# Routing records that leave the order of visits to the reader, with memsets of 128x256 words between the scatters

## The chip, the cores and the metric

One core of one Trainium2 chip runs the whole program. The metric is device time in microseconds (us) per run; fewer is better. A profiled execution is a run of its own with the hardware profiler on: its span goes from the first to the last instruction, and its own time lies a little above the span.

## The reference, cut to what matters

Two layers follow each other. The first is attention over keys and values that are averaged in groups of 8, the second a mixture of 8 experts, of which each token visits two.

```python
def _attn_ref(q, k, v):                      # q, k, v: (8, 8, 576, 64)
    k_p = k.reshape(B, H, Sp, pool, D).mean(axis=3)      # pool = 8, Sp = 72
    v_p = v.reshape(B, H, Sp, pool, D).mean(axis=3)
    scores = scale * np.matmul(q, k_p.transpose(0, 1, 3, 2))
    attn = softmax(scores)
    return np.matmul(attn, v_p)

def _moe_ref(x, w_gate, w_noise, noise, w1, w2):   # x: (4608, 512), E, F = 8, 1024
    noisy_logits = x @ w_gate + np.log1p(np.exp(x @ w_noise)) * noise
    top2 = the two largest of noisy_logits per token
    top2_w = softmax over these two
    for e in range(E):
        for k in range(2):
            mask = top2[:, k] == e
            h = np.maximum(x[mask] @ w1[e], 0.0)
            out[mask] += top2_w[mask, k, None] * (h @ w2[e])

reference: x = attention output as (4608, 512); out = _moe_ref(x, ...)
```

## The kernel before

**Attention and router.** The 8 batches are taken as 4 pairs of 1152 tokens each. A pair's x rows are stored in `x_dram`, and while the next pair's attention runs, the router `route` (L506 to L676) works out the top two experts of the pair before: their weights, and for each choice its position in the expert's list (L629 casts it). It then writes a record of four words per choice into `rec_dram`: the number of the x row, the weight, the row of `out` or a number out of bounds (L647), and the slot of the other visit (L643). Here each token's visits have an order: only the second one, in the order of the experts, adds the first one's result, which lies in `slot_dram`, and writes the sum to `out`. The dozen operations at L630 to L647 find that order from both choices.

**Scatters.** A pair has 9 columns of 128 tokens and two choices, so 18 indirect DMAs (`scatter`, L649) of 128 records each, on GpSimd's queue (POOL). They are kept in a list, `scq`, in program order with what follows them: the loading of records (`load_recs`, L678) and the gathers of x rows (`fetch`, L744). `advance(n, m)` (L794) takes m of them from the list at places in the attention and in the first groups of the experts, and ties them to a recent instruction (`pace`). `quiet` keeps some of these places free. `spaced` (L496) puts a memset of `spacer`, 128x512 words, between any two indirect DMAs:

```python
            with tc.issue_after(tail_ind[0].ins):
                gap = nc.gpsimd.memset(spacer[0], 0.0)
            with tc.issue_after(gap.ins):
                tail_ind[0] = make()
```

For the last scatters the memsets go to the buffer `lg3`, which has the same size.

**Experts.** An expert's list is cut into groups of up to four tiles of 128 tokens. For expert 0 they are tiles 0 to 3 (group 0), 4 and 5 (group 1) and 6 to 9 (group 2); group 3 is the first of expert 1. Group 0 needs records of pairs 0 and 1 alone, group 1 those up to pair 2, group 2 those up to pair 3, so these three are loaded apart, as `raw0_0`, `raw0_4` and `raw0_6`, and all records of experts 1 to 7 as `raw1_0`. The first two of these loads go out on POOL, the rest on SP's queue, which also carries the x rows and the weight loads `wst` (L459). The list `scq` has, after pair 2's scatters, `raw0_4` and the gathers of group 1, then pair 3's scatters, `raw0_6` and the gathers of group 2.

Each group runs through the same steps. Its rows are gathered (`xg`, L718) and transposed (on PE for expert 0, L768) and split into a high and a low part (`split`); stage 1 multiplies by w1 (L1030, with L1041 on ScalarE and L1042 on VectorE, which split h again), stage 2 by w2 (L1141 for expert 0, or L1107) tile by tile. Then `finish` scales a tile's rows by the weight (L1080, L1078) into one of three buffers `pv` and stores them in `slot_dram` (L1082, on POOL) or scatters them to `out` (L1086). The split of the next group stands after a tile of the group's stage 2, by `hook` (L1178): after tile 1 - i of group i. In front of the groups' code three memsets fill the `pv` buffers (L981).

**Engines.** PE is TensorE, DVE is VectorE, ACT is ScalarE, POOL is GpSimd, SP is SyncE. Each runs its own queue in order; the order is that of the program, with the pins of `issue_after`.

## Time and profile before

| What | Value |
| --- | --- |
| median of 3 runs | 1026.51 us (1026.15 to 1030.2) |
| profiled execution, its own time | 1030.06 us |
| its span | 1028.1 us |
| PE busy | 994.1 us (97%) |
| PE weight loads | 890.1 us (87%) |
| DVE busy | 551.6 us (54%) |
| ACT busy | 345.0 us (34%) |
| POOL busy | 415.1 us (40%) |
| chain that ended last, PE's share | 79% |

The profiled execution is 3.55 us above the median. Busy times are sums over the span; work on different engines overlaps. A wait in the timeline is the idle time ahead of an instruction with what released it. The attention ends at about 190 us; from there the program is the groups of the experts one after another.

### The profile page before, as it was taken

Reading aid. Unit: us, or ns where it says so; the run is one execution under the profiler, and the core shown is the slowest. Engines: PE = TensorE matmul, PEld = TensorE weight load, DVE = VectorE, ACT = ScalarE, POOL = GpSimd, SP = SyncE. Lnnn points to the kernel's source line nnn. Section 1 sums busy time; section 2 is a strip of 40 time slices with the busy share of each in tenths; the row PEclk is TensorE's granted clock in tenths of the full one; section 3 lists DMA queues with packets and bytes.
Section 4 is the critical chain, followed back from the end, with each engine's and each line's share of the span. In section 5 each row is a group of like instructions: output and inputs, shape, how many; then the busy total and the mean of one; then the engine's idle time right before and its main releaser. Section 6 shows DMA issues by size and latency. Waiting matters only on the chain.

```text
span 1028.1 us, 16525 instructions
## 1 busy us (share of the span) xinstructions
PE 994.1 (97%) x5832; PEld 890.1 (87%) x5832; DVE 551.6 (54%) x1283; ACT 345.0 (34%) x857; POOL 415.1 (40%) x494
## 2 busy tenths in 40 slices
PE   7999999988899999999999999999999999999996
PEld 6798998867798988898988898989888988898995
DVE  5699988932245454644454446344544455456341
ACT  4687788521113222421232124212321232123120
POOL 4023878968500442155215421552154215422514
PEclk9899999989899999999999999999999999999999
DMA  9986954441707765676267746772677357744623
GB/s 279 341 272 222 321 187 129 142 134 27 222 35 212 205 183 148 192 245 193 76 175 242 216 125 209 243 212 74 184 241 232 114 170 245 244 145 135 210 88 135
DMA packets 137382, 190.36 MB, mean 185 GB/s; under 512 B 29155, under 2 KB 84084, under 8 KB 137274
## 3 DMA queue, kind: packets, MB, share of 16 engines
q1 hardware_dynamic: 111834, 121.84, 39.3%
q0 software_dynamic: 25440, 67.05, 21.2%
q8 instruction: 72, 1.18, 0.5%
q14 instruction: 36, 0.29, 0.1%
HBM read 126.07 MB, written 70.74 MB: 191 GB/s over the span
## 4 chain that ended last, share of the span: by engine, by line
PE 79%; DMA 6%; DVE 5%; POOL 4%; issue 3%; ACT 2%; SPq 1%; POOLq 0%; DVEq 0%; ACTq 0%
PE bank L1030 32%; PE bank L1141 23%; PE bank L1107 10%; PE a L408 5%; PE s L375 3%; PE ep L393 2%; DMA wst<-in_moe_w_dram 2%; PE qp L347 1%; POOL rec_dram L650 1%; DVE w L481 1%; POOL lg L501 1%; DMA v<-in_v_dram 1%; ACT ex L382 1%; POOL out_dram L1086 1%; DMA tab_dram<-tab 1%
## 5 line engine op out<-in xcount | busy, mean ns | idle before, releaser
L1030 PE MATMUL bank<-xh,w 128*128 128x512 f32 (+6 forms) x1536 | 390.6, 338 | 2.1 <-DVE pv L1080 1.5
L1030 PEld LDWEIGHTS bank<-xh,w 128*128 128x128 f32 x1536 | 270.3, 188 | 22.9 <-DVE pv L1080 1.7
L1141 PE MATMUL bank<-w,hh 128*128 128x512 f32 x880 | 273.9, 393 | 0.0
L1030 PE MATMUL bank<-xl,w 128*128 128x512 f32 (+6 forms) x768 | 259.7, 338 | 0.0
L1041 ACT ACTIVATE hh<-bank 128x512 fp32r<-128x512 f32 (+4 forms) x192 | 97.5, 510 | 468.7 <-PE bank L1030 444.6
L1042 DVE SCALAR_TENSOR_TENSOR hl<-bank,hh 128x512 fp32r<-128x512 f32 (+4 forms) x192 | 110.9, 579 | 241.1 <-ACT hh L1041 241.1
L1141 PEld LDWEIGHTS bank<-w,hh 128*128 128x128 f32 x880 | 166.7, 190 | 34.4
L1141 PE MATMUL bank<-w,hl 128*128 128x512 f32 x440 | 172.4, 392 | 0.0
L1030 PEld LDWEIGHTS bank<-xl,w 128*128 128x128 f32 x768 | 144.6, 188 | 10.3
L1082 POOL DMA_DIRECT2D slot_dram<-yt x17 | 9.8, 574 | 266.2 <-DVE yt L1078 218.5
L1078 DVE SCALAR_TENSOR_TENSOR pv<-bank,raw,pv 128x128 f32<-128x128 f32 x196 | 55.5, 343 | 107.0 <-PE bank L1141 58.0
L1107 PE MATMUL bank<-hh,w 128*128 128x240 f32 (+3 forms) x512 | 104.7, 300 | 2.0 <-issue 2.0
L1141 PEld LDWEIGHTS bank<-w,hl 128*128 128x128 f32 x440 | 83.3, 189 | 17.5
L1062 POOL DMA_INDIRECT pv<-slot_dram,raw x70 | 68.6, 980 | 67.9 <-DMA slot_dram<-ys 35.0
L650 POOL DMA_INDIRECT rec_dram<-rec,pos x72 | 81.1, 1127 | 36.7 <-DVE rd L415 24.5
L481 DVE TENSOR_TENSOR w<-wst,w 128x512 fp32r<-128x512 f32 x128 | 82.5, 683 | 10.4 <-ACT w L480 10.4
L1107 PEld LDWEIGHTS bank<-hh,w 128*128 128x128 f32 x512 | 83.9, 192 | 2.2 <-issue 2.2
L727 POOL DMA_INDIRECT row<-x_dram,raw x70 | 71.1, 1016 | 24.7 <-issue 20.0
L480 ACT CAST w<-wst 128x512 fp32r<-128x512 f32 x128 | 72.9, 619 | 22.7 <-DMA wst<-in_moe_w_dram 22.6
L1082 POOL DMA_DIRECT2D slot_dram<-pv x55 | 31.7, 576 | 117.4 <-DVE pv L1078 93.7
L1107 PE MATMUL bank<-hl,w 128*128 128x320 f32 (+3 forms) x256 | 76.5, 299 | 0.0
L382 ACT ACTIVATE ex<-s,mx 128x72 f32<-128x72 f32 x288 | 70.5, 345 | 8.0 <-DVE mx L380 7.8
(167 smaller groups left out, 1073.0 us busy)
## 6 DMA issues: line engine op xcount, KB each, us to landing
wst<-in_moe_w_dram SPq DMA_DIRECT2D x64, 512.0 KB
via<-row SPq DMA_DIRECT2D x266, 64.0 KB
xg<-via SPq DMA_DIRECT2D x63, 256.0 KB
slot_dram<-pv POOLq DMA_DIRECT2D x55, 256.0 KB
k<-in_k_dram SPq DMA_DIRECT2D x7, 1280.0 KB
v<-in_v_dram SPq DMA_DIRECT2D x16, 512.0 KB
x_dram<-xr SPq DMA_DIRECT2D x16, 512.0 KB
q<-in_q_dram SPq DMA_DIRECT2D x7, 1024.0 KB
```

What stands on the lines that cost most here:

```text
L382: lasta[0] = nc.scalar.activation(ex[:, jj, EPOS[h] * G:(EPOS[h] + 1) * G], sv[:, i], AF.Exp, bias=mx[:, i:i + 1])
L480: nc.scalar.copy(hv, sv)
L481: nc.vector.tensor_sub(lv, sv, hv.bitcast(F32))
L650: s = spaced(lambda: nc.gpsimd.indirect_dma_start(out=rec_dram[:, :], out_offset=bass.IndirectOffsetOnAxis(ap=pos[:, i, c:c + 1], axis=0), ...
L727: turn_of("pool", lambda: nc.gpsimd.indirect_dma_start(out=row[:32 * nr], out_offset=None, in_=x_dram[:, :], in_offset=bass.IndirectOffset ...
L1030: nc.tensor.matmul(part(ph), w1s(e, a, db, f), part(xs[b][:, db]), start=(i == 0), stop=(i == 3 * NDB - 1))
L1041: act = nc.scalar.activation(hh[:, :n], ph[:, :n], AF.Relu)
L1042: last = nc.vector.scalar_tensor_tensor(hl[:, :n], ph[:, :n], 0.0, hh[:, :n].bitcast(F32), op0=OP.max, op1=OP.subtract)
L1062: turn_of("pool", lambda: nc.gpsimd.indirect_dma_start(out=pv[:np_], out_offset=None, in_=slot_dram[:P + e * CAP, :], in_offset=bass.Indir ...
L1078: nc.vector.scalar_tensor_tensor(r_, y_, wc, pv[:plain] if plain else r_, op0=OP.mult, op1=OP.add)
L1107: nc.tensor.matmul(part(py), w2s(e, b, f)[:, mb * P:(mb + 1) * P], part(hs[f][a]), start=(i == 0), stop=(i == 3 * NFB - 1))
L1141: mm = nc.tensor.matmul(py, hs[f][a][:, cs], w2s(e, b, f), start=(i == 0), stop=(i == 3 * NFB - 1))
```

## The change

Four things are done.

1. The memset between indirect DMAs is half as long, and the gathers of expert 0's tiles from 4 on have none (`queued`).
2. The records carry the sum of both positions and the sum of both experts instead of the out row and the mate's slot. A reader knows its own expert and place, takes them off, and finds the order of visits. Expert 0 needs none of it, since its visit is always the first. For experts 1 to 7 it is worked out once for all (`second_visits`, 13 DVE operations on 128x70 words, ahead of group 3), from `own_places` (four iotas early in the program). The overflow loop at the end, which isn't run with these inputs, does it for itself.
3. The load `raw0_4` goes out on SP and `raw0_6` on POOL, the gathers of group 1 stand behind the fourth scatter of pair 3 instead of ahead of the first, and the split of group 1 after tile 2 of group 0 instead of tile 1.
4. `quiet` is gone, so scatters also go out at the places that it kept free; the memsets of `pv` are gone, and `mb`'s is done once.

```diff
         nc.gpsimd.memset(pad[:, :, 2:3], int(BIG))
+        nc.gpsimd.memset(pad[:, :, 3:4], 8 * E)
         nc.sync.dma_start(rec_dram.rearrange("(p r) c -> p r c", p=P), pad)
...
             with tc.issue_after(tail_ind[0].ins):
-                gap = nc.gpsimd.memset(spacer[0], 0.0)
+                gap = nc.gpsimd.memset(spacer[0][:, :DM // 2], 0.0)
             with tc.issue_after(gap.ins):
...
         return tail_ind[0]
+
+    def queued(make):
+        with tc.issue_after(tail_ind[0].ins):
+            tail_ind[0] = make()
+        return tail_ind[0]
+
+    mb = rp.tile([P, NCH + 1, E], BF16, name="mb")
+    nc.vector.memset(mb[:, NCH:], 0.0)
...
             ms.append(m)
-        mb = rp.tile([P, NCH + 1, E], BF16, tag="mb", name=f"mb{pr}_{c0}")
-        V.memset(mb[:, n:], 0.0)
         V.tensor_add(mb[:, :n], ms[0], ms[1])
...
         V.tensor_scalar(word(0), tb, float(pr * 2 * S), None, op0=OP.add)
+        both = [P, 2, n]
+        V.scalar_tensor_tensor(word(3), ei[:, 0].unsqueeze(1).to_broadcast(both), 2.0 * E,
+                               ei[:, 1].unsqueeze(1).to_broadcast(both), op0=OP.add, op1=OP.add)
         W = n * E
...
         V.tensor_copy(pos[:, :, :n], pf)
-        key = t(2, NCH)
-        V.scalar_tensor_tensor(key, ei, -float(ER), pf, op0=OP.mult, op1=OP.add)
-        V.tensor_scalar(key, key, float(CAP + E * ER), float(E), op0=OP.is_ge, op1=OP.mult)
-        jump = t(2, NCH)
-        V.tensor_scalar(jump, ei, float((OVR - CAP) // E), float((OVR - CAP) + (E - 1) * CAP // E),
-                        op0=OP.mult, op1=OP.add)
-        V.tensor_mul(jump, jump, key)
-        V.tensor_add(jump, jump, pf)
-        slot = t(2, NCH)
-        V.scalar_tensor_tensor(slot, ei, -float(OVR), jump, op0=OP.mult, op1=OP.add)
-        V.tensor_add(key, key, ei)
-        later = t(2, NCH)
-        for i in range(2):
-            V.tensor_tensor(later[:, i], key[:, i], key[:, 1 - i], op=OP.is_gt)
-            V.scalar_tensor_tensor(word(3)[:, i], slot[:, 1 - i], float(P - E * OVR), later[:, i],
-                                   op0=OP.add, op1=OP.mult)
-        V.tensor_scalar(later, later, -BIG, BIG + float(pr * 2 * S), op0=OP.mult, op1=OP.add)
-        V.tensor_add(word(2), later, tb)
+        V.tensor_add(word(2), pf[:, 0].unsqueeze(1).to_broadcast(both), pf[:, 1].unsqueeze(1).to_broadcast(both))
...
                 scq.append(lambda c=c, i=i: scatter(c, i))
+            if pr == NP - 1 and c == 1:
+                scq.append(lambda: fetch(groups[1]))
         if pr == NP // 2 - 1:
...
             scq.append(lambda: load_recs(0, 1, 1, 2, 2))
-            scq.append(lambda: fetch(groups[1]))
         if pr == NP - 1:
...
             scq.append(lambda: load_recs(1, E, 0, 4))
+
+    def visits(t, words, selfp, es, keys, mate_, tok_):
+        V = nc.vector
+        po, eo, ro, la, ju = (t(i) for i in range(5))
+        V.tensor_sub(po, words(2), selfp)
+        V.tensor_sub(eo, words(3), es)
+        V.scalar_tensor_tensor(ro, eo, -float(ER), po, op0=OP.mult, op1=OP.add)
+        V.tensor_single_scalar(ro, ro, float(CAP), op=OP.is_ge)
+        V.scalar_tensor_tensor(la, ro, float(E), eo, op0=OP.mult, op1=OP.add)
+        V.tensor_tensor(la, keys, la, op=OP.is_gt)
+        V.tensor_scalar(ju, eo, float(OVR - CAP), float((E - 1) * CAP), op0=OP.mult, op1=OP.add)
+        V.tensor_mul(ju, ju, ro)
+        V.tensor_add(ju, ju, po)
+        V.scalar_tensor_tensor(ju, eo, -float(OVR), ju, op0=OP.mult, op1=OP.add)
+        V.scalar_tensor_tensor(mate_, ju, float(P), la, op0=OP.add, op1=OP.mult)
+        V.tensor_scalar(la, la, -BIG, BIG, op0=OP.mult, op1=OP.add)
+        return V.tensor_add(tok_, la, words(0))
+
+    raws = {}
+    selfp = cp.tile([P, E - 1, SECT[-1][0] + 1], F32, name="selfp")
+
+    def own_places():
+        for ts, n, np_ in SECT:
+            nc.gpsimd.iota(selfp[:, :, ts:ts + n], pattern=[[ER, E - 1], [1, n]], base=ER + ts * P,
+                           channel_multiplier=n, allow_small_or_imprecise_dtypes=True)
+
+    def second_visits():
+        ne, nt = E - 1, SECT[-1][0] + 1
+        raw = raws[1]
+
+        def t(i):
+            return rp.tile([P, NCH, E], F32, tag=f"rt{i + 2}", name=f"sv{i}").rearrange(
+                "p n e -> p (n e)")[:, :ne * nt].rearrange("p (e t) -> p e t", e=ne)
+
+        der = rp.tile([P, 2, ne, nt], I32, name="der")
+        es = eidx[:, 1:].unsqueeze(2).to_broadcast([P, ne, nt])
+        visits(t, lambda w: raw[:, :, :, w], selfp, es, es, der[:, 0], der[:, 1])
+        for e in range(1, E):
+            for t_ in range(nt):
+                mate[e, t_] = der[:, 0, e - 1, t_:t_ + 1]
+                tokc[e, t_] = der[:, 1, e - 1, t_:t_ + 1]
...
             V.memset(raw[64:, :, nt - 1, :], 0)
+        raws[e0] = raw
         src = rec_dram.rearrange("(e r) c -> e (r c)", e=E)
...
             o = ts * P * RW
-            ld = (nc.gpsimd if RE >> (0 if early else 1 if e0 == 0 else 2) & 1 else nc.sync).dma_start(raw[:np_, :, ts - t0:ts - t0 + n].rearrange("p e t c -> p e (t c)"),
+            ld = (nc.gpsimd if e0 == 0 and early != 2 else nc.sync).dma_start(raw[:np_, :, ts - t0:ts - t0 + n].rearrange("p e t c -> p e (t c)"),
                                    src[e0:e1, o:o + np_ * n * RW].rearrange("e (p x) -> p e x", p=np_))
...
                 xi[e, t] = raw[:, i[0], i[1], 0:1]
-                tokc[e, t] = raw[:, i[0], i[1], 2:3]
-                mate[e, t] = raw[:, i[0], i[1], 3:4]
                 wcol[e, t] = raw.bitcast(F32)[:, i[0], i[1], 1:2]
...
         if e == 0:
-            g = spaced(lambda: nc.gpsimd.indirect_dma_start(
+            g = (spaced if t < 4 else queued)(lambda: nc.gpsimd.indirect_dma_start(
                 out=xg, out_offset=None, in_=x_dram[:XT0 if t < 4 else NTOK, :],
...
     plan(6, pad_recs)
+    plan(6, own_places)
     plan(20, zero_rows)
...
         eT = None
-        quiet = 0 if ci == 0 and pr <= NP // 2 or ci == NCH - 1 and pr < NP // 2 else 1
-
         def bgs():
...
             pace[0] = lastx[0]
-            advance(STEPS[pr], 2 * quiet if pr >= NP // 2 else quiet)
+            advance(STEPS[pr], 2 if pr >= NP // 2 else 1)
...
                         pace[0] = lasta[0]
-                        advance(0, quiet)
+                        advance(0, 1)
             elif ui + 2 < NU:
...
         t = mp.tile([P, DM], F32, name=f"pv{i}")
-        nc.gpsimd.memset(t, 0.0)
         pvb.append(t)
...
     def hook(i, t, mm):
-        if t == 1 - i:
+        if t == 2 - 2 * i:
             with tc.issue_after(mm.ins):
...
                 count(e)
+        if i == NG:
+            with tc.issue_after(pace[0].ins):
+                second_visits()
         if i == NG + 1:
             with tc.issue_after(pace[0].ins):
-                tot, tabr = over_table()
+                tot, tabr, tab_dram = over_table()
         stage1(g, (lambda f: hook1(i, f)) if i < 2 else flush if i == len(groups) - 1 else None)
```

On POOL, the end of pair 2 and the start of pair 3. `rec2` and `rec3` are their records, `raw0_4` those that group 1 reads, `xg0_4` and `xg0_5` group 1's rows. Before:

```order
L650 DMA rec_dram_68<-rec2_0_2332,pos2_0_2475 37376x4
L501 MEMSET lg3_2171 128x512
L691 DMA raw0_4_2847<-rec_dram_68 128x8
L718 DMA xg0_4_2849<-x_dram_67,raw0_4_2847 128x512
L501 MEMSET lg3_2171 128x512
L718 DMA xg0_5_2852<-x_dram_67,raw0_4_2847 128x512
L501 MEMSET lg3_2171 128x512
L650 DMA rec_dram_68<-rec3_0_2909,pos3_0_2987 37376x4
```

And after, from the third scatter of pair 3 on:

```order
L642 DMA rec_dram_68<-rec3_0_2855,pos3_0_2934 37376x4
L501 MEMSET lg3_2145 128x256
L642 DMA rec_dram_68<-rec3_0_2855,pos3_0_2934 37376x4
L751 DMA xg0_4_2968<-x_dram_67,raw0_4_2801 128x512
L751 DMA xg0_5_2970<-x_dram_67,raw0_4_2801 128x512
L501 MEMSET lg3_2145 128x256
L642 DMA rec_dram_68<-rec3_0_2855,pos3_0_2934 37376x4
```

The gathers have moved behind four scatters of pair 3, without memsets of their own, and the load of `raw0_4` is no longer in this queue.

On SP, around the last store of x rows (`xr3_7_1_0`); `wst0_3_1` is the last quarter of expert 0's w2, `wst1_...` are expert 1's. Before:

```order
L429 DMA x_dram_67<-xr3_7_1_0_2760 128x1024
L459 DMA wst0_3_1_2958<-in_moe_w2_dram 128x2x512
L459 DMA wst1_0_0_3027<-in_moe_w1_dram 128x1024
L459 DMA wst1_0_1_3055<-in_moe_w1_dram 128x1024
L459 DMA wst1_1_0_3283<-in_moe_w1_dram 128x1024
```

After:

```order
L429 DMA x_dram_67<-xr3_7_1_0_2717 128x1024
L726 DMA raw0_4_2801<-rec_dram_68 128x8
L459 DMA wst0_3_1_2905<-in_moe_w2_dram 128x2x512
L459 DMA wst1_0_0_2958<-in_moe_w1_dram 128x1024
L459 DMA wst1_0_1_2988<-in_moe_w1_dram 128x1024
```

The load of group 1's records stands ahead of the weight loads.

On POOL, the end of pair 3, after the change (before, the two loads of `raw0_6` are on SP, and a memset stands ahead of each gather):

```order
L642 DMA rec_dram_68<-rec3_0_2855,pos3_0_2934 37376x4
L1113 DMA slot_dram_69<-pv1_2774 128x512
L726 DMA raw0_6_3112<-rec_dram_68 128x12
L726 DMA raw0_6_3112<-rec_dram_68 64x4
L751 DMA xg0_6_3116<-x_dram_67,raw0_6_3112 128x512
L751 DMA xg0_7_3118<-x_dram_67,raw0_6_3112 128x512
L751 DMA xg0_8_3120<-x_dram_67,raw0_6_3112 128x512
L751 DMA xg0_9_3122<-x_dram_67,raw0_6_3112 128x512
L1113 DMA slot_dram_69<-pv2_2775 128x512
```

The records of group 2 are loaded on the queue that wrote them, and its four gathers follow each other directly.

## Rows read from the trace of the kernel before

**Rows 1.** By windows: start:end, us, busy us and count of PE, PEld, DVE, ACT, POOL, PEclk, DMA share, GB/s
```profile
100.00:135.00 35.00, 35.00 (x315) 32.34 (x314) 32.23 (x109) 28.07 (x100) 26.18 (x30) 1.00 0.89 268
218.60:236.60 18.00, 14.71 (x56) 11.95 (x57) 3.64 (x10) 1.17 (x2) 16.17 (x23) 0.81 0.12 32
250.00:272.70 22.70, 16.89 (x66) 13.02 (x65) 4.05 (x9) 2.52 (x5) 13.68 (x18) 0.77 0.63 165
306.00:360.00 54.00, 54.00 (x255) 46.58 (x254) 28.37 (x70) 15.00 (x28) 14.29 (x17) 1.00 0.72 209
```
**Rows 2.** Waits of PE, whole span: what waited <- for what: us in total, times, longest us
```profile
PE bank L768 <- DMA xg<-x_dram,raw: 9.2, 6, 3.7
...
PE bank L1030 <- DVE pv L1080: 1.5, 1, 1.5
```
**Rows 3.** Timeline of PE: start us, us, engine line op tile xcount [idle before <- releaser]
```profile
207.51 0.62 PE L1141 MATMUL bank<-w,hh 128*128 128x512 f32 x2
...
221.36 1.13 PE L768 MATMUL bank<-ident,xg 128*128 128x128 f32 x4 [2.81 <-DMA xg<-x_dram,raw]
...
236.64 0.28 PE L1030 MATMUL bank<-xh,w 128*128 128x256 f32 x1
...
246.60 0.28 PE L1030 MATMUL bank<-xh,w 128*128 128x256 f32 x1
...
259.26 1.13 PE L768 MATMUL bank<-ident,xg 128*128 128x128 f32 x4 [3.71 <-DMA xg<-x_dram,raw]
```
**Rows 4.** The chain that ended last, in order of time: start us, us, what
```profile
178.36 1.23 PE xp L768 x8
...
260.74 3.96 DMA xg<-x_dram,raw
...
272.74 16.42 PE bank L1030 x96
...
430.17 21.76 PE bank L1141 x96
```
**Rows 5.** Timeline of POOL, 168 to 245 us
```profile
168.17 0.59 POOL L691 DMA_DIRECT2D raw<-rec_dram  x1 [0.87 <-DMA rec_dram<-rec,pos]
...
177.30 1.27 POOL L650 DMA_INDIRECT rec_dram<-rec,pos  x1 [0.17 <-issue]
...
213.69 0.58 POOL L691 DMA_DIRECT2D raw<-rec_dram  x1 [2.89 <-DMA rec_dram<-rec,pos]
217.97 1.01 POOL L718 DMA_INDIRECT xg<-x_dram,raw  x1 [3.70 <-DMA wst<-in_moe_w_dram]
...
244.22 0.59 POOL L1082 DMA_DIRECT2D slot_dram<-pv  x1
```
**Rows 6.** Groups of POOL by shape (busy us, mean ns); tile rec_dram (ns min/median/max, first, last start)
```profile
L501 POOL MEMSET spacer<- 128x512 f32 x55 | 29.8, 542 | 0.0
...
masks.py:197 POOL MEMSET ident<- 128x128 f32 x1 | 0.2, 205 | 0.3 <-POOLq L1323 0.3
...
L650 POOL DMA_INDIRECT rec_dram<-rec,pos x72: 973/977/2304, 91.8 to 250.6; - x72
```
**Rows 7.** Timeline of DVE: positions (L629), last record word (L647), half-split, weight split
```profile
127.64 0.20 DVE L629 CAST pos<-rt 128x18 int32<-128x18 f32 x1
...
133.85 0.18 DVE L647 TENSOR_TENSOR rec<-rt,tok 128x18 int32<-128x18 f32 x1
...
167.41 0.18 DVE L629 CAST pos<-rt 128x18 int32<-128x18 f32 x1
...
191.24 0.68 DVE L1042 SCALAR_TENSOR_TENSOR hl<-bank,hh 128x512 fp32r<-128x512 f32 x1
...
200.12 0.41 DVE L629 CAST pos<-rt 128x18 int32<-128x18 f32 x1
...
204.41 0.68 DVE L481 TENSOR_TENSOR w<-wst,w 128x512 fp32r<-128x512 f32 x1
```
**Rows 8.** Timeline of SP's queue, 196 to 198 us
```profile
197.12 0.37 SPq L459 DMA_DIRECT2D wst<-in_moe_w_dram  x1
```

More of the change, by code (lines that the diff above doesn't have):

```diff
@@ L131 @@
     H0 = 80
-    RE = 1
     PT = dict(zip(('kT', 'vTp', 'vr'), [{'o': 'one', 's': 's'}[c] for c in 'ooo']))
@@ L1230, in over_table @@
         nc.sync.dma_start(tabr, tab_dram.rearrange("(o a) c -> o (a c)", o=1))
-        return tot, tabr
+        return tot, tabr, tab_dram
     for i, g in enumerate(groups):
@@ L1278 @@
         nc.sync.dma_start(w2t, moe_w2[bass.ds(er, 1)].rearrange("o (c p) m -> p (o c) m", p=P))
+        at = op.tile([P, 3], I32, name="oat")
+        nc.sync.dma_start(at, tab_dram[bass.ds(it, 1), :].to_broadcast([P, 3]))
+        oself = op.tile([P, 1], F32, name="oself")
+        nc.vector.tensor_add(oself, prow, at[:, 0:1])
+        okey = op.tile([P, 1], F32, name="okey")
+        nc.vector.tensor_scalar(okey, at[:, 1:2], float(E), None, op0=OP.add)
+        oto = op.tile([P, 2], I32, name="oto")
+        visits(lambda i: op.tile([P, 1], F32, name=f"ov{i}"), lambda w: rec[:, w:w + 1], oself,
+               at[:, 1:2], okey, oto[:, 0:1], oto[:, 1:2])
         xg = op.tile([P, DM], F32, name="oxg")
@@ L1286 @@
             out=pv, out_offset=None, in_=slot_dram[:, :],
-            in_offset=bass.IndirectOffsetOnAxis(ap=rec[:, 3:4], axis=0))
+            in_offset=bass.IndirectOffsetOnAxis(ap=oto[:, 0:1], axis=0))
         xp = ops.tile([P, NDB, P], F32, name="oxp")
@@ L1306 @@
         nc.gpsimd.indirect_dma_start(
-            out=out, out_offset=bass.IndirectOffsetOnAxis(ap=rec[:, 2:3], axis=0),
+            out=out, out_offset=bass.IndirectOffsetOnAxis(ap=oto[:, 1:2], axis=0),
             in_=res, in_offset=None, bounds_check=NTOK - 1, oob_is_err=False)
```

## The prediction

> **What bounds the kernel now.** I read the page first: TensorE (PE) is busy for 97% of the span, so time can only come from stretches in which PE stands or runs slow. The table by windows finds them. In 306 to 360 us PE is busy for all 54.00 us at a granted clock of 1.00; in 100 to 135 us (attention) for all 35.00 [rows 1]. The two windows from 218.60 and from 250.00 are different: 14.71 of 18.00 us at a clock of 0.81, and 16.89 of 22.70 us at 0.77 [rows 1]. The waits of PE name what ends these pauses: the transposes of L768 wait 9.2 us in 6 places for expert 0's gathered x rows, and stage 1 waits 1.5 us once for the scale of L1080 [rows 2]. PE's timeline puts them in one place: 2.81 us at 221.36 and 3.71 at 259.26 are the longest, all in the second stage of group 0 and the two stages of group 1 [rows 3]. Behind each pause PE runs at the lower of its two levels for a while (0.81 and 0.77 are means over both).
>
> So the stretch runs from 207.51, where stage 2 of group 0 begins [rows 3], to 272.74, where stage 1 of group 2 begins [rows 4]: 65.23 us. The same work at full speed without waits is:
> - 144 matmuls of 512 columns at 21.76/96 = 0.227 us [rows 4]: 32.6 us
> - 96 of 256 columns: 84 of them lie between 236.64 and 246.60, so 0.12 us each with the last one's end [rows 3]: 11.5 us
> - 24 transposes at 1.23/8 = 0.154 us [rows 4]: 3.7 us
>
> Together 47.8 us. The stretch holds 65.23 - 47.8 = 17.4 us, of which 10.7 are waits [rows 2] and 6.7 the slow clock behind them.
>
> Why the rows are late is read on POOL. One queue does 1. pair 2's 18 scatters, 2. group 1's records and gathers, 3. pair 3's 18 scatters, 4. group 2's gathers. Pair 2's first scatter starts at 177.30, the record load waits until 213.69 for the last to land, and the first gather starts at 217.97 [rows 5]; the last scatter of pair 3 starts at 250.6 [rows 6]. The store of group 1's scaled rows stands in the same queue and goes out at 244.22 only [rows 5]: this is the wait of 1.5 us, since the next scale waits for its buffer.
>
> **The change, part by part.** *Shorter memset.* 128x512 takes 542 ns and 128x128 takes 205 [rows 6]; 128x256 lies between. On the straight line through both it is 0.32 us, which I take: the two rows bound it closely. A scatter takes 977 ns in the median [rows 6] and 0.17 us of issue stand ahead of each [rows 5], so a spaced scatter goes from 1.68 to about 1.46 us.
>
> *Records.* Today pair 2's positions are cast at 167.41 and pair 3's at 200.12 [rows 7]; then some dozen small DVE operations make the other words, about 0.18 us each and mixed with other work. After the change one addition follows the cast. Scatters can start at about 168 and 200.7. POOL must be there too: today it is still loading records at 168.17 and starts pair 2 at 177.30 [rows 5]. Pair 1's 18 scatters gain 18 x 0.22 = 4 us by the memset, and their records some 6 us: today the positions are there at 127.64 and the last word at 133.85, in a later step of the router [rows 7]. So the load at 168.17 comes some 10 us earlier, and group 0's gathers, 9 us from there to 177.30, are out before 168. With the 4 us alone pair 2 would start some 5 us later.
>
> *Pair 2.* Sixteen scatters from 168 take 16 x 1.46 = 23.4 us; the 17th is tied to the half-split of group 0's first part, done at 191.92 [rows 7], and so is not held. The 18th ends at about 194.5. Records landed 1.4 us (before the load at 168.17) to 3.4 us (before that at 213.69) after their scatter's end, so they are there at 196 to 198.
>
> *Group 1's records move from POOL to SP.* The load stands ahead of the weight load that goes out at 197.12 today [rows 8], and what is queued behind it are all later weight loads. That first one was cast and split at 205.09 [rows 7], 8.0 us after its issue. PE needs it at the last quarter of group 0's first output tile, 207.51 + 0.75 x 5.44 = 211.6. With L for the landing of pair 2's last record and 0.6 us for the load's issue [rows 5], PE waits L + 0.6 + 8.0 - 211.6 = L - 203. At L of 196 to 198 this costs nothing, with 5 us of cover, which the later start of pair 2 would just use up.
>
> *Gathers of group 1* now stand behind four scatters of pair 3: 200.7 + 4 x 1.46 = 206.5. The records are there by 202.4 (198 plus the 4.28 us between load and gather at 213.69 and 217.97). Two gathers, without memsets and so in no more than 1.46 us each, end by 209.4; a gather landed 3.96 us after its start [rows 4], so the rows are there by 212 to 213. The split that needs them moves one tile later, to 207.51 + 3 x 5.44 = 223.8. Group 1's waits of 2.81 us and what follows go.
>
> *Pair 3 and group 2.* Fourteen scatters from 209.6, with one store between, end at about 230.6. The store that goes out at 244.22 now comes at about 223, so the wait of 1.5 us goes. The load of group 2's records (now on POOL) waits for the last landing, 231.5 to 234; gathers begin 4.28 us later as those of group 1 do today, the fourth 3 x 1.46 behind the first, and with 3.96 for it to land the rows are there at 244 to 247. PE wants them at 207.51 + 21.76 + 1.2 + 11.5 + 5.44 = 247.4. This is the thinnest margin, 0 to 3 us. If it holds, group 2's waits go: 9.2 less 2.81, at most 6.4 us.
>
> *With the waits the slow clock goes.* Both slow windows begin with such a pause; 236.64 to 246.60 ran at full speed. I count all 6.7 us.
>
> *At nothing:* fewer DVE operations and shorter memsets in attention lie beside a PE that is busy for 35.00 of 35.00 us [rows 1]; if that cover is thin, they give back up to three pairs x 11 x 0.18 = 5.9 us, the low end. The 13 operations that work out the visits for experts 1 to 7 run once on 128x70 words, at most about 0.25 us each (between a 128x18 cast and a 128x512 split, 0.18 and 0.68 us [rows 7]), so 3.3 us on DVE beside stage 2 of group 2, where DVE has about half its time free [rows 1]; without that cover the cost is 3.3 us. The iotas and one more memset lie on POOL before its first scatter at 91.8 [rows 6].
>
> **Sum.** The execution profiled took 1030.06 us; less 17.4 it gives 1012.7. The median of the runs is 1026.51, 3.5 us lower, so there I expect 1009.
>
> **Rivals.** *B, group 2 stays late.* The scatters last from 973 to 2304 ns [rows 6], the long ones while DVE works, and where the memset isn't what sets the period, halving it doesn't shorten it. At 1.68 us each the 32 scatters ahead of group 2's gathers end 7 us later, beyond the margin. For it: the long scatters in attention; against: from 207 to 250 their median is the minimum. It gives back up to 6.4 us of group 2's waits and half of the slow clock, 3.3: up to 1009 + 9.7 = 1018.7, with 1012 where the rows are late by 1 or 2 us. The Trainium skill, "SBUF — State Buffer", section "Who interferes with whom", says that DVE and GpSimd hold a shared port in turns, for a whole instruction each, and that a DMA issued by GpSimd waits for it; by that rule B would be what happens, and the median here speaks against it.
>
> *C, SP is held.* Today POOL stood idle for 2.89 us before the record load at 213.69 [rows 5], and its next work waited behind it. On SP the weight loads would stand so. If pair 2's last record landed as late as today, at about 213.7, PE would wait 213.7 - 203 = 10.7 us and run slow for some 3.3: 1009 + 14 = 1023, no change. For it: the change does put the load ahead of the weights; against: pair 2's scatters would have to gain nothing from a start 9 us earlier. The Trainium skill, "DMA: Bandwidth & Descriptors", section "Anatomy of one DMA", says that a DMA's semaphore wait is made on the sequencer that issues it; the 2.89 us agree, and by it each us of L beyond 203 would cost one.
>
> *D, slower,* is the same place further on: 17.4 us are used up and 5.1 more (0.5%, about what a measurement of this kernel can tell from no change) lost when L - 203 + 3.3 passes 22.5, at L over 222. The time would be 1032 to 1036. Only a pair 2 that starts later than today would do it; nothing in the rows points there.
>
> *That the change doesn't do what it says* would be B again: gathers that come earlier than today but not early enough.
>
> **Numbers.** Forecast 0.75 (1003 to 1012), B 0.16 (1012 to 1019), C 0.06, D 0.03. The range takes forecast and B: 1003 to 1019. Faster 0.91, the same (1021.4 to 1031.6) 0.06, slower 0.03.
>
> **What the new profile would show.** If right: memsets of about 0.32 us; group 1's first gather at about 207 and group 2's at 235 to 240; no wait of the transposes for gathered rows over 0.5 us; clock 1.00 from 207 to 256; stage 1 of group 2 begins near 255 in place of 272.74; a store of scaled rows near 223; the first weight load behind the record load by 199. Wrong for B if transposes of group 2 wait near 247; for C if PE stops near 211.6 for weights; and the forecast is too high if attention itself ends earlier than today.

## The result, and the profile after

The changed kernel took 1016.91 us in the median of 4 runs (1014.09 to 1021.21), the kernel before in the same comparison 1027.88 (1026.15 to 1030.2): a ratio of 0.9895, with a 95% interval of 0.9852 to 0.9939. It is faster, by 11 us or 1%. The forecast was 1009, which was 17.4 us below a median of 1026.51 over three of these four runs of the kernel before. The profiled execution took 1014.09 us, with a span of 1012.0 against 1028.1. One of the runs that are compared further on, of `gap512`, took 1094.7 us at a mean granted clock of 0.85 and is not in its ratio.

I start with the chain of the changed kernel, from the last part of stage 1 of group 0 on (columns as in [rows 4]):

```profile
200.58 11.00 PE bank L1061 x48
211.57 16.32 PE bank L1172 x72
227.90 0.96 PE bank L801 x8
228.85 5.49 PE bank L1172 x24
234.35 11.51 PE bank L1061 x96
245.86 5.47 PE bank L1172 x24
251.33 1.92 PE bank L801 x16
253.25 5.48 PE bank L1172 x24
258.73 16.42 PE bank L1061 x96
```

Nothing but PE stands in it, piece after piece: no gather, no store, no scatter, as there were before [rows 4]. The 8 transposes of group 1 take 0.96 us and the 16 of group 2 take 1.92, 0.12 us each. Stage 1 of group 2 begins at 258.73 instead of 272.74. The windows say the same (columns as in [rows 1]):

```profile
86.00:190.00 104.00, 95.50 (x799) 85.23 (x798) 85.30 (x253) 79.65 (x268) 77.39 (x106) 1.00 0.62 191
211.40:258.70 47.30, 47.30 (x266) 41.58 (x265) 16.63 (x41) 9.32 (x21) 32.42 (x45) 1.00 0.55 156
```

In the stretch that the prediction is about, PE is busy for all 47.30 us at a clock of 1.00, where the two windows of before had 0.81 and 0.77 [rows 1]. But in attention, 86 to 190 us, it is busy for 95.50 us only; in the same window of the kernel before it was 101.45:

```profile
86.00:190.00 104.00, 101.45 (x850) 91.76 (x850) 92.93 (x309) 83.96 (x287) 81.57 (x96) 1.00 0.66 202
```

So something was lost there. Two events of attention measure it: the fourth and the last reciprocal of L415, on the timeline of DVE. First before, then after:

```profile
46.28 0.19 DVE L415 RECIPROCAL rd<-rd 128x8 f32<-128x8 f32 x1
...
185.92 0.19 DVE L415 RECIPROCAL rd<-rd 128x8 f32<-128x8 f32 x1
```

```profile
42.54 0.19 DVE L415 RECIPROCAL rd<-rd 128x8 f32<-128x8 f32 x1
...
189.88 0.19 DVE L415 RECIPROCAL rd<-rd 128x8 f32<-128x8 f32 x1
```

With these two, the first matmul of stage 2 of group 0 (207.51 [rows 3]; 211.41 on the timeline after) and the start of stage 1 of group 2 the spans divide as follows. The third column is the changed kernel in a second profile, of which more below.

| Stretch, us | before | after | after, again |
| --- | --- | --- | --- |
| start to the fourth reciprocal | 46.28 | 42.54 | 43.77 |
| attention: to the last reciprocal | 139.64 | 147.34 | 140.28 |
| to stage 2 of group 0 | 21.59 | 21.53 | 21.53 |
| to stage 1 of group 2 (the stretch) | 65.23 | 47.32 | 47.31 |
| to the end of the span | 755.36 | 753.27 | 754.11 |
| span | 1028.1 | 1012.0 | 1007.0 |

The stretch gave back 17.9 us, for which the forecast was 17.4. Attention took 7.7 us more, and the start 3.7 less. The start differs with the clock in these two executions; first before, then after:

```profile
20.00:40.00 20.00, 18.28 (x130) 16.49 (x130) 11.87 (x24) 11.30 (x38) 0.00 (x0) 0.76 1.09 335
```

```profile
20.00:40.00 20.00, 18.17 (x157) 15.74 (x158) 15.02 (x31) 14.22 (x49) 0.00 (x0) 1.00 1.09 341
```

Between 20 and 40 us, ahead of the first scatter, the granted clock was 0.76 before and 1.00 after. Over all profiles of this study it lies between 0.74 and 1.00 there, and the fourth reciprocal at 42.5 to 48.1 us; in the changed kernel's second profile it was 0.94, so the change doesn't set it.

On POOL the steps of the prediction stand one by one (columns as in [rows 5]):

```profile
158.59 0.59 POOL L726 DMA_DIRECT2D raw<-rec_dram  x1 [1.45 <-DMA rec_dram<-rec,pos]
...
168.24 1.01 POOL L642 DMA_INDIRECT rec_dram<-rec,pos  x1 [0.17 <-issue]
...
197.62 0.98 POOL L642 DMA_INDIRECT rec_dram<-rec,pos  x1 [0.16 <-issue]
...
204.79 0.97 POOL L642 DMA_INDIRECT rec_dram<-rec,pos  x1 [5.86 <-DVE rec L639]
...
211.06 0.99 POOL L751 DMA_INDIRECT xg<-x_dram,raw  x1 [0.30 <-issue]
...
227.61 0.59 POOL L1113 DMA_DIRECT2D slot_dram<-pv  x1
...
237.08 1.10 POOL L726 DMA_DIRECT2D raw<-rec_dram  x2 [1.13 <-DMA rec_dram<-rec,pos]
240.92 1.03 POOL L751 DMA_INDIRECT xg<-x_dram,raw  x1 [2.73 <-PE bank L1061]
```

Group 0's records are loaded at 158.59 instead of 168.17, pair 2 starts at 168.24 instead of 177.30 and its last scatter at 197.62, group 1's first gather goes out at 211.06 instead of 217.97, the store at 227.61 instead of 244.22 [rows 5]. Everything after pair 2's start stands some 4 us later than forecast, because attention itself is late: the first scatter of pair 3 waits 5.86 us for its records, at 204.79. In the second profile, with a short attention, group 1's first gather goes out at 205.46 and group 2's at 235.29, where 207 and 235 to 240 were forecast. On SP, group 1's records are loaded here, which puts L, their landing, at 199.75:

```profile
199.75 0.34 SPq L726 DMA_DIRECT2D raw<-rec_dram  x1
```

The memsets, in the groups by shape:

```profile
L501 POOL MEMSET spacer<- 128x256 f32 x55 | 18.0, 328 | 0.1
```

### The profile page after: what moved, and what is told of

Read it like the earlier page. It is cut to its first block, busy times and chain, and to the rows that moved or that the text cites. A ratio compares the mean times of both kernels' runs of the same rounds, so it can differ in the third digit from the quotient of the medians.

```text
span 1012.0 us, 16487 instructions
## 1 busy us (share of the span) xinstructions
PE 984.8 (97%) x5832; PEld 881.2 (87%) x5832; DVE 549.5 (54%) x1249; ACT 344.7 (34%) x857; POOL 396.1 (39%) x491
## 4 chain that ended last, share of the span: by engine, by line
PE 84%; DVE 4%; DMA 3%; issue 3%; ACT 2%; POOL 1%; SPq 1%; another core or an unknown queue 0%; POOLq 0%; DVEq 0%; ACTq 0%
PE bank L1061 37%; PE bank L1172 26%; PE bank L1138 10%; PE a L408 4%; PE ep L393 2%; PE s L375 2%; PE qp L347 1%; DMA v<-in_v_dram 1%; ACT ex L382 1%; DMA tab_dram<-tab 1%; POOL out_dram L1117 1%; DVE k L233 1%; PE s L365 0%; ACT eT L395 0%; PE kT L298 0%
## 5 line engine op out<-in xcount | busy, mean ns | idle before, releaser
L1072 ACT ACTIVATE hh<-bank 128x512 fp32r<-128x512 f32 (+4 forms) x192 | 97.2, 508 | 459.7 <-PE bank L1061 394.5
L1093 POOL DMA_INDIRECT pv<-slot_dram,der x70 | 68.4, 978 | 67.8 <-DMA slot_dram<-ys 35.2
```

The costliest lines, as they stand in the source:

```text
L1072: act = nc.scalar.activation(hh[:, :n], ph[:, :n], AF.Relu)
L1093: turn_of("pool", lambda: nc.gpsimd.indirect_dma_start(out=pv[:np_], out_offset=None, in_=slot_dram[:P + e * CAP, :], in_offset=bass.Indir ...
```

## The experiments

Two questions are open. What of the change brings the 18 us, and what are the 7 us in attention? Every run was compared with the kernel before. Where a ratio is given its interval is the 95% one. "Attention" is always the time from the fourth to the last reciprocal, and "the stretch" that from stage 2 of group 0 to stage 1 of group 2. Some totals are of a single execution.

### Records alone

`records_only` is the kernel before with the new records and `second_visits`; all else of the change is undone, except that `mb`'s memset is still done once. Against the changed kernel, lines cut short:

```diff
-gap = nc.gpsimd.memset(spacer[0][:, :DM // 2], 0.0)
+gap = nc.gpsimd.memset(spacer[0], 0.0)
...
-if pr == NP - 1 and c == 1:
-    scq.append(lambda: fetch(groups[1]))
...
+scq.append(lambda: fetch(groups[1]))
...
-(nc.gpsimd if e0 == 0 and early != 2 else nc.sync)
+(nc.gpsimd if early else nc.sync)
...
-(spaced if t < 4 else queued)
+spaced
...
+quiet = 0 if ci == 0 and pr <= NP // 2 or ci == NCH - 1 and pr < NP // 2 else 1
...
+nc.gpsimd.memset(t, 0.0)
...
-if t == 2 - 2 * i:
+if t == 1 - i:
```

> The kernel before with the new records and the visits worked out by the reader, and nothing else of the change (full memsets, queues, quiet places and pv memsets as before). Attention is measured from the fourth to the last reciprocal of the attention (L415): 139.6 us before, 147.3 after the change; the stretch from stage 2 of group 0 to stage 1 of group 2: 65.2 before, 47.2 after. If the records' edit alone makes attention longer, by the other order in which the scheduler then puts attention's instructions on PE, ACT and DVE: 146 to 148 in attention. If the closer scatters or the freed quiet places do it: 139 to 141. The stretch: pair 2's scatters start about 6 us earlier by the earlier records of pair 1, and PE comes later, so some of the waits go: 48 to 56. Total against before: ratio 0.995 to 1.000 by the first, 0.985 to 0.992 by the second.

Measured: ratio 0.9964 (0.9941 to 0.9987), 1027.65 us. Attention took 140.4 us and the stretch 65.3, from 205.65 to 270.95, and the waits of PE in it are those of before [rows 2]:

```profile
PE bank L800 <- DMA xg<-x_dram,raw: 8.6, 6, 3.7
PE bank L1063 <- DVE pv L1113: 2.5, 1, 2.5
```

So the records alone bring nothing in the stretch, where 48 to 56 us were expected, although pair 2 starts 4 us earlier (at 173.53). The records' edit does change the order in which PE, ACT and DVE run attention's instructions. That other order costs nothing: my first theory for the 7 us falls.

### All but the records, full memsets, quiet places

`no_records` is the kernel before with the rest of the change, but it keeps the memsets of `pv` and does `mb`'s each time. Against the changed kernel:

```diff
-V.tensor_add(word(2), pf[:, 0].unsqueeze(1).to_broadcast(both), pf[:, 1].unsqueeze(1).to_broadcast(both))
+key = t(2, NCH)
...
+V.tensor_add(word(2), later, tb)
```

> The kernel before with all the rest of the change (memsets of 128x256, no quiet places, the loads and gathers in their new queues and places, group 1's split after tile 2), but with the old records and their dozen DVE operations. If the records' edit lengthens attention: 139 to 141 us here, and 1006 to 1014 us in all with a stretch of 48 to 53 (records of pairs 1 to 3 come 4 to 6 us later than after the change, so group 2's rows are late by 0 to 3 us). If scatters or quiet places lengthen it: 146 to 148 and 1014 to 1022 in all.

`full_memset` is the changed kernel with one line as before:

```diff
-gap = nc.gpsimd.memset(spacer[0][:, :DM // 2], 0.0)
+gap = nc.gpsimd.memset(spacer[0], 0.0)
```

> The changed kernel with memsets of 128x512 between the scatters, as before. If the halving is what lets group 2's rows come in time: the 18 scatters of pair 3 end 4 us later and the transposes of group 2 wait 1 to 3 us, with slow clock behind them; the stretch is 49 to 52. If the earlier records and the queues are enough: 47 to 48, and the same time as after the change. Attention: 147 by the theory of the other order; 140 to 144 if the denser scatters are what disturbs it.

`quiet_back` is the changed kernel with the quiet places:

```diff
+quiet = 0 if ci == 0 and pr <= NP // 2 or ci == NCH - 1 and pr < NP // 2 else 1
...
-advance(STEPS[pr], 2 if pr >= NP // 2 else 1)
+advance(STEPS[pr], 2 * quiet if pr >= NP // 2 else quiet)
...
-advance(0, 1)
+advance(0, quiet)
```

> The changed kernel with the quiet places back, so that no scatter goes out in the first and last chunks that were kept free. By the theory of the other order attention stays at 147 and the total at the changed kernel's 1014 to 1018; if scatters at those places delay attention, 140 to 142, and 1007 to 1011 in all. The stretch should be 47 to 49 either way, since pair 2 and pair 3 keep their places.

Measured:

| Kernel | total, median | ratio | attention | stretch |
| --- | --- | --- | --- | --- |
| no_records | 1024.37 | 0.9953 (0.9924 to 0.9982) | 156.7 | 47.3 |
| full_memset | 1018.65 | 0.9899 (0.9858 to 0.994) | 140.2 | 52.8 |
| quiet_back | 1016.42 | 0.9877 (0.9837 to 0.9918) | 146.8 | 47.3 |

Attention is long in the two kernels with 128x256 and short in the two with 128x512: that looked like an effect of the memsets, and not of the quiet places. The 156.7 us of `no_records` lie outside both of its expectations; its attention also ran at a mean clock of 0.95. The short stretch of `no_records` says little, since PE came there 14 us later than before (at 221.68), and the rows had that time as well.

`full_memset` shows rival C, not the waits for group 2's rows that were expected. Its pair 2 ends late, and the record load on SP goes out at 203.86 only:

```profile
203.86 0.34 SPq L726 DMA_DIRECT2D raw<-rec_dram  x1
204.31 17.13 SPq L459 DMA_DIRECT2D wst<-in_moe_w_dram  x8
```

The weight loads behind it are late, ACT waits for them, and a half of stage 1 that PE needs (L1072) stands behind the weight casts in ACT's queue. The timeline of ACT, and then that of PE:

```profile
209.04 1.14 ACT L480 CAST w<-wst 128x512 fp32r<-128x512 f32 x2 [8.58 <-DMA wst<-in_moe_w_dram]
210.35 1.14 ACT L480 CAST w<-wst 128x512 fp32r<-128x512 f32 x2 [0.17 <-DMA wst<-in_moe_w_dram]
211.39 0.59 ACT L1072 ACTIVATE hh<-bank 128x512 fp32r<-128x512 f32 x1
```

```profile
212.04 0.73 PE L1172 MATMUL bank<-w,hh 128*128 128x512 f32 x2 [2.69 <-ACT hh L1072]
213.00 0.56 PE L1172 MATMUL bank<-w,hl 128*128 128x512 f32 x1 [0.23 <-DVE hl L1073]
213.76 0.80 PE L1172 MATMUL bank<-w,hh 128*128 128x512 f32 x1 [0.20 <-ACT hh L1072]
```

The prediction's price was L - 203 with stage 2 of group 0 at 207.51. Here that stage began at 205.11, 2.4 us earlier, so the price is 203.86 - 200.6 = 3.3 us. The three waits make 3.12 us. With the slow clock that follows (0.74 in the 6.5 us from 211.5) the stretch costs 52.80 - 47.31 = 5.5 us more than after the change.

### Four widths of the memset in attention

`gap512` takes the load of group 1's records back to POOL and gives the memsets of the attention's own buffer (55 of them) a width of their own; the later ones stay at 256. The other three differ from it in the width alone (`gap768` by a second memset of 256 words behind the first).

```diff
+gw = [512]
...
-gap = nc.gpsimd.memset(spacer[0][:, :DM // 2], 0.0)
+gap = nc.gpsimd.memset(spacer[0][:, :gw[0]], 0.0)
...
-ld = (nc.gpsimd if e0 == 0 and early != 2 else nc.sync).dma_start(...
+ld = (nc.gpsimd if e0 == 0 else nc.sync).dma_start(...
...
 spacer[0] = lgs[NP - 1][:, :4].rearrange("p j h c -> p (j h c)")
+gw[0] = DM // 2
```

> The changed kernel with memsets of 128x512 while they go to the attention's own buffer (55 of them), 128x256 as changed for the rest, and the load of group 1's records back on POOL. Attention, from the fourth to the last reciprocal of L415, was 147.3 us after the change and 140.2 with full memsets everywhere. If the halving in attention is the loss: 139.5 to 141 here. If the wait of 2.9 us that PE had with full memsets came from the record load that held the weight loads on SP (it went out at 203.9), it is gone now, and the stretch from the last reciprocal to stage 1 of group 2 is 68 to 70 us (74.3 with full memsets, 68.9 after the change). Then the total is 3 us below the full memsets' and 5 to 8 below the changed kernel's: 1008 to 1013. If ACT's wait had another cause: 2 to 3 us of wait stay.

> As gap512 with memsets of 128x384 in the attention, a scatter every 1.57 us or so. If the rate of the scatters is what lengthens attention: between the two, 141 to 146. If 128x256 only met an unlucky order: 139.5 to 141 or over 147, with no order in the widths.

> As gap512 with memsets of 128x128 in the attention, a scatter every 1.34 us. By the rate: 149 to 158 in attention. By an unlucky order: anything, 140 as likely as 150.

> As gap512 with two memsets, 128x512 and 128x256, in the attention, a scatter every 2.1 us. By the rate: 139 to 140.5 in attention, as good as without any effect of scatters; by an unlucky order: not told. Pair 2's scatters end later, by 18 x 0.4 = 8 us or more, so group 1's records and with them both stages behind come late, and the waits are back: 3 to 12 us in the stretch.

Measured:

| Kernel | total | attention | stretch |
| --- | --- | --- | --- |
| gap512 | 1015.91 median, ratio 0.9889 (0.9861 to 0.9917) | 140.2 | 56.2 |
| gap384 | 1018.59 (one) | 141.7 | 53.3 |
| gap128 | 1011.52 (one) | 141.6 | 47.3 |
| gap768 | 1032.82 (one) | 150.1 | 65.8 |

The rate of the scatters alone isn't it either: with 128x128 they follow each other faster than after the change (1.36 us from start to start in pair 1, for 1.47, in the median), and attention is short. The 150.1 of `gap768` has a plain cause, group 0's own gathers come too late for attention's end (timeline of PE; its stretch has 10.7 us of waits for gathered rows, as before the change):

```profile
181.70 1.10 PE L805 MATMUL xp<-ident,xg 128*128 128x128 f32 x4 [6.61 <-DMA xg<-x_dram,raw]
```

`gap512` was to be the best of all, and its expectation failed in another place. C is gone: PE waits for no weights. But the record load on POOL now holds pair 3's scatters until pair 2's records have landed, and group 2's rows are late. Timeline of POOL, then of PE:

```profile
208.84 0.58 POOL L727 DMA_DIRECT2D raw<-rec_dram  x1 [4.36 <-DMA rec_dram<-rec,pos]
209.72 0.99 POOL L643 DMA_INDIRECT rec_dram<-rec,pos  x1 [0.31 <-issue]
...
244.47 1.03 POOL L752 DMA_INDIRECT xg<-x_dram,raw  x1 [2.01 <-issue]
```

```profile
247.94 1.13 PE L802 MATMUL bank<-ident,xg 128*128 128x128 f32 x4 [2.87 <-DMA xg<-x_dram,raw]
249.44 1.13 PE L802 MATMUL bank<-ident,xg 128*128 128x128 f32 x4 [0.37 <-DMA xg<-x_dram,raw]
250.78 1.13 PE L802 MATMUL bank<-ident,xg 128*128 128x128 f32 x4 [0.21 <-DMA xg<-x_dram,raw]
253.18 1.13 PE L802 MATMUL bank<-ident,xg 128*128 128x128 f32 x4 [1.27 <-DMA xg<-x_dram,raw]
```

This is the place of rival B, reached by another cause than longer scatters: 4.7 us of waits, and with the clock (0.70 from 244.00 to 261.30) 56.16 - 47.31 = 8.9 us in the stretch; the prediction had 9.7 as the most that it could cost. `gap384` loses in the same place, with 3.6 us of waits. With either queue for the load, memsets of 384 or 512 words in attention cost 5 to 9 us in the stretch, because pair 2 ends late: its last scatter ends 1.0 to 4.1 us ahead of stage 2 of group 0 in these three kernels, and 11.0 to 12.8 us in the two profiles of the changed kernel.

### The same kernel again, and the width by itself

After these, two things were left for the 7 us: the width of 256 itself (long in three of three kernels that have only it), or chance of an execution.

`after_again` has no edit. `gap256` and `gap128_again` are the kernel above with another number:

```diff
-gw = [512]
+gw = [256]
```

> The changed kernel once more, nothing edited, for one more profile. Attention, from the fourth to the last reciprocal, took 147.3 us in its first profile, 146.8 and 156.7 in the two other kernels with 128x256 memsets in attention, and 139.6 to 141.7 in six profiles with 128x128, 128x384 or 128x512 (with 128x512 and 128x256 after each other it was 150.1, but there group 0's gathers came 6.6 us late). If the loss belongs to the width: 146 to 149 again, with stretches in which PE, ACT and DVE stand at once. If it is chance of a single execution: 140 to 142 as likely.

> As gap128 and gap512, with 128x256 in the attention too (and the record load of group 1 on POOL); the four differ in this one number. If the loss belongs to the width: 146 to 149 in attention. If chance: 140 to 142.

> gap128 once more, timed: memsets of 128x128 in the attention, 128x256 for the rest, group 1's record load on POOL. Attention 140 to 142 as in its first look, no wait of the transposes for gathered rows, and a total of 1008 to 1012 us, 5 to 8 below the changed kernel, if the width of 256 is the loss; 1013 to 1017 as the changed kernel's if attention's length is chance.

`before_half` is the kernel before, with:

```diff
-gap = nc.gpsimd.memset(spacer[0], 0.0)
+gap = nc.gpsimd.memset(spacer[0][:, :DM // 2], 0.0)
```

> The kernel before with the memsets halved and nothing else, so the instructions of PE, ACT and DVE stand in the same order as before. If the loss belongs to the width: 146 to 157 in attention against 139.6. If chance: 139 to 142. The stretch: pair 3's scatters end 4 us earlier and pair 2's 3 to 5, so of 10.7 us of waits 3 to 7 go.

Measured:

| Kernel | total | attention | stretch |
| --- | --- | --- | --- |
| after_again | 1009.02 (one) | 140.3 | 47.3 |
| gap256 | 1013.35 (one) | 141.6 | 47.3 |
| gap128_again | 1010.96 median, ratio 0.983 (0.98 to 0.9859) | 141.6 | 47.3 |
| before_half | 1018.52 (one) | 139.5 | 55.3 |

The changed kernel itself, with nothing edited, has a short attention in its second profile:

```profile
43.77 0.19 DVE L415 RECIPROCAL rd<-rd 128x8 f32<-128x8 f32 x1
...
184.05 0.19 DVE L415 RECIPROCAL rd<-rd 128x8 f32<-128x8 f32 x1
```

```profile
86.00:190.00 104.00, 100.77 (x831) 90.92 (x831) 89.96 (x271) 82.32 (x278) 79.31 (x109) 1.00 0.65 200
205.60:252.90 47.30, 47.30 (x267) 41.59 (x265) 16.32 (x41) 9.06 (x20) 32.69 (x45) 1.00 0.54 153
```

PE is busy for 100.77 us in the window where it was busy for 95.50 in the first, and the total is 1009.02 us. `before_half` and `gap256` have the width of 256 and a short attention too. So the width alone doesn't decide it, nor does anything else of the change that I could take away; the same program has a long attention in one execution and a short one in another. The total of `gap128_again` lies where its expectation put it if the width were the loss, but the other three runs speak against that. That the width makes a long attention more likely isn't excluded: of six profiles with memsets of 128x256 alone three are long, of seven with another single width none.

What the long ones look like, in the first profile of the changed kernel, 155 to 158 us, on PE, on ACT and on DVE:

```profile
156.40 0.60 PE L347 MATMUL qp<-ident,q 128*128 128x128 f32 x4
157.72 0.51 PE L317 MATMUL vTp<-ident,vs 112*128 112x112 f32 x3 [0.72 <-ACT eT L395]
```

```profile
155.28 0.28 ACT L302 ACTIVATE kbd<-kT 64x144 f32<-64x144 f32 x1
157.30 0.37 ACT L395 COPY eT<-ep 112x256 f32<-112x256 f32 x1 [1.74 <-PE qp L347]
```

```profile
155.47 0.23 DVE L556 TENSOR_TENSOR rt<-rt,rt 128x72 f32<-128x72 f32 x1
157.38 0.46 DVE L380 TENSOR_REDUCE mx<-s 128x4 f32<-128x288 f32 x1 [1.69 <-PE qp L347]
```

ACT and DVE stand from 155.6 and 155.7 until 157.3, and from 157.0 PE does too: 0.3 us with all three idle. Taking every stretch of over 0.15 us in which all three stand, from the 13th to the last reciprocal, I find 1.0 us in this profile, 1.6 in `quiet_back` and 3.5 in `no_records`, the three with a long attention (in `gap768` it is the wait for gathers); in the ten others there is none. The waits of PE in attention in `no_records` are mostly put down to "issue", nothing that the profile shows:

```profile
PE s L375 <- issue: 2.5, 1, 2.5
...
PE vTp L317 <- issue: 1.6, 1, 1.6
```

The trace also has the times at which semaphores were updated, the signals by which an engine tells another that it is done; the timelines don't show them. PE's five updates for matmuls that ended between 155.41 and 157.00 all stand between 157.27 and 157.49, the first of them 1.86 us late, and ACT and DVE, which waited for them, go on at 157.30 and 157.38. Most of the other pauses end with such a late burst of PE's updates too. Why they come late isn't shown.

There is a rival that no run here excludes, the recording itself. In the traces of these three executions 12 to 13% of the semaphore updates of PE, DVE, ACT and POOL are missing, and 11 to 12% in those of `records_only` and `full_memset`, which have 128x512 and a short attention; the other nine traces have all of them or all but a few, and no such pauses. So the pauses were seen only where memsets of 128x256 and a trace with missing updates came together.

It stays open what decides whether an execution has such pauses, and whether the other three timed runs of the changed kernel had them. Their spans suggest it: 1014.0 to 1019.3 us at mean clocks of 0.991 to 0.993, where the second profile had 1007.0 us at 0.991.

### What of the change brings the 18 us

Halving the memsets alone takes the stretch from 65.2 to 55.3 us, with 4.9 us of waits for gathered rows left (`before_half`), so it brings 9.9. All but the halving brings 12.4 (`full_memset`, 52.8). Both together bring 17.9, less than the sum. `gap256` is the changed kernel with group 1's record load back on POOL, and its stretch is 47.3 as well, so with these memsets the move of that load to SP brings nothing there. What the earlier records, the moved gathers and the freed quiet places bring one by one isn't shown; the records by themselves bring nothing.

## Why the prediction was right, and by how much it was off

- **The bound and the sum.** Right for the stretch. 47.8 us of work was left in it by the forecast; it took 47.3, so 17.9 us came back for 17.4. Both waits and all of the slow clock went, as counted. The 24 transposes took 2.9 us, not 3.7, which was read from transposes in attention.
- **The total.** Luck has a part in it. 1016.91 lies in the range, but not in the forecast's own part (1003 to 1012): it lies in the part for rival B (1012 to 1019), and B did not happen, since group 2's rows came in time. The forecast was a change of 17.4 us, the medians show 11.0, and what is lacking is of the size of the loss in attention.
- **Shorter memset.** Forecast 0.32 us, measured 0.328. It carries weight: with 384 or 512 words in attention the stretch is 5 to 9 us longer (`full_memset`, `gap512`, `gap384`). By itself, in the old queues, it brought 65.2 - 55.3 = 9.9 us (`before_half`).
- **Records.** Pair 2's first scatter was forecast at about 168 and came at 168.24 and 168.19. The records' edit alone brought nothing in the stretch (`records_only`). That it pays together with faster scatters isn't shown: in `no_records`, the kernel that could tell, attention was late and gave the rows time.
- **Record load on SP.** L was forecast at 196 to 198 with 5 us of cover. In the second profile the load went out at 196.22, 4.9 us ahead of the limit (203 less the 1.9 us by which stage 2 began earlier); in the first, with attention late, the cover was 7. The price L - 203 held in `full_memset` to 0.2 us. What PE waited for there was, by its timeline, not the weights, as I had it, but a half of stage 1 behind the weight casts in ACT's queue, so that the size fits is partly luck. And the move itself was not needed (`gap256` has the same 47.3 us without it). The Trainium skill, "DMA: Bandwidth & Descriptors", section "Anatomy of one DMA", has it that the issuing sequencer waits, not the DMA engine; the SP rows of `full_memset` agree, with the weight loads behind the record load, from 204.31 on.
- **Group 2.** The thinnest margin held. In the second profile the last of its four gathers starts at 239.16 and lands near 243 at 3.96 us, and PE transposes from 245.50: some 2 us, for 0 to 3 forecast. `gap512` shows the other side, at 8.9 us.
- **Rival B by a longer scatter.** The spaced scatters of pair 2 run from 168.19 to 193.58 in the second profile, 25.39/17 = 1.49 us each, for 1.46 forecast. So halving does shorten the period. The Trainium skill, "SBUF — State Buffer", section "Who interferes with whom", lets DVE and GpSimd block each other fully where DVE runs in a two-port mode, a condition that the prediction left out. Which mode DVE was in during these 18 scatters isn't shown; they took 975 ns in the median and 1202 at most, so none waited long.
- **Attention at nothing.** This is the term that was off in the first result. "At nothing" was argued from a busy PE, with a possible gain; I had no loss in it. The first profile lost 7.7 us there, the second 0.6. The median of 1016.91 against 1009 is of that size. The second profile's 1009.02 is the forecast, but a single execution, and I had not allowed for attention's length to differ between executions.
- **After the stretch.** 2.1 and 1.3 us less than before, not forecast; half of it is a PE idle time of 2.56 us in 360 to 400 us before that is 1.5 and 1.9 us in the same work after; the rest I did not follow.

Of the kernels tried, `gap128` is the fastest that was timed: 0.983 (0.98 to 0.9859), below the changed kernel's 0.9895 (0.9852 to 0.9939). Its stretch is the same 47.3 us, and its attention has no pauses in two profiles. The intervals overlap, and the changed kernel without pauses ran in 1009.02 us, so that it is better by its own doing isn't shown.

## What to carry to other kernels

In a queue in order, price a moved wait by what stands behind it and from which time on it counts (here L - 203), and shift that time with the consumer's own start; in `full_memset` the price then fitted to 0.2 us. Don't add up what parts of a change bring alone: 9.9 us by the halving and 12.4 by all the rest made 17.9 together, and one step, the load on SP, wasn't needed for it. Take a second profile of the same program before you explain a difference in a part that the change hardly touches: here the order of the instructions, the rate of the scatters and the width of a memset each seemed to explain 7 us that came and went with the same program. And see whether both traces are complete.

## What was not expected of the hardware

- PE, ACT and DVE stood at the same time, for 0.3 to 1.1 us at a go, in three of the fourteen profiles, all with semaphore updates missing from the trace; in the pause at 157.0 PE's updates came up to 1.86 us late. Attention was then 7 to 17 us longer (147.3, 146.8 and 156.7 against 139.5 to 141.7).
- At the start of the program, between 20 and 40 us, the granted clock was 0.74 to 1.00 in different executions, and the fourth reciprocal lay at 42.5 to 48.1 us, the latest where the clock was 0.74.
- Records were ready for their load between 1.1 us (at 199.75 after the change, whose last scatter ended at 198.60) and 4.7 us (at 208.84 in `gap512`, whose last scatter ended at 204.16) behind the end of the last scatter.
